# Sliding-window attention and a highway layer on one core: the order of issue changed at seven steps

## Chip, core and metric

The kernel runs on one core of a Trainium2 chip. The metric is the device time of one execution in microseconds (us); a lower time is better. Engines are named as in the profile: PE (TensorE), DVE (VectorE), ACT (ScalarE), POOL (GpSimd) and SP (SyncE). POOL and SP also issue the DMAs.

## What is computed

Attention with a causal window of 128 positions and an ALiBi bias, for 8 batches, 8 heads, 576 positions and 64 dimensions, then a highway layer on the 4608 x 512 result. Inputs and output are float32.

```python
scores = scale * np.matmul(q, k.transpose(0, 1, 3, 2))
mask = (rel >= 0) & (rel < window)                 # rel = query - key position, window = 128
scores = np.where(mask, scores + bias[None], -1e9) # bias = -slope(head) * |rel|
attn = exp(scores - max) / sum
x = attn @ v                                       # heads side by side: 4608 x 512
H = np.maximum(x @ w_h, 0.0)
T = 1.0 / (1.0 + np.exp(-(x @ w_t + b_t)))
out = T * H + (1.0 - T) * x
```

## The kernel before

**Attention** is done in 32 units (batch b, s, g): s picks heads 0 to 3 or 4 to 7, g the first or second half of the query tiles. A unit is six steps, each with a letter that the order string uses:

- `T` (line 184, DVE): transposes of q and of k, from the loaded buffer `ld` into `tr`. T (b, s, 0) is q, T (b, s, 1) is k, for both halves g.
- `s` (line 227, PE): scores into four PSUM banks. Always banks 0 to 3, so a unit's scores wait for the exponential of the unit before.
- `e` (line 244, ACT): exponential, PSUM to `p` in bf16.
- `m` (line 249, DVE): the mask product, `p` times exp(bias) with zeros outside the window. For three units the bias is added by PE instead (line 209).
- `p` (lines 260 to 281, PE): PV, the product with V and a column of ones, into two halves of a PSUM bank pair named in the string (4 or 6).
- `n` (lines 294 and 295, DVE): the normalisation, reciprocal and product, PSUM to `x`. It frees the banks that the PV step filled.

**The highway layer** is done in 36 blocks (b, i) of 128 rows; i is 0 to 3, and 4 in odd batches, for the first 64 rows of two batches. Its steps:

- `x` (321, PE) four transposes of `x` into PSUM, `c` (326, ACT) their copy to `xt`, `h` (331, PE) the product with w_h.
- `u` (DVE): relu and the subtraction of x, `uu` = max(h, 0) - x, from PSUM (347, "relu-sub" below). For 14 blocks ACT does the relu first (`r`, 338) and DVE subtracts in SBUF (344). It frees the bank of h.
- `z` (355, 357, PE) the product with w_t and the bias; for 12 blocks ACT puts the bias in PSUM (`w`, 368) and PE adds to it (`y`, 372).
- `a` (377, ACT) tanh; then 0.5 + 0.5 tanh, on ACT (`t`, 381) or for 11 blocks on DVE (`k`, 385, the "half-gate").
- `g` (390, DVE): the gate product, `uu` times the gate.
- `o` (394, POOL): the sum with x into `ot`; for two blocks on DVE (`q`, 399). `d` (406, 410, SP) stores it.

**Loads** (`L`, lines 130, 136, 140, 144) are all issued by POOL and turn float32 into bf16. A load ("t", b, s, w) brings q (w = 0) or k (w = 1) of four heads into one of 20 `ld` buffers. A load ("v", b, 2, tile) brings 128 key positions of V of batches b and b + 1, all heads, into `va`. PV of half g = 0 reads V tiles 0 to 2, that of g = 1 tiles 1 to 4. POOL does its sums and its load issues in one order.

**What sets the order.** A string written out by hand, `ORDER`, gives every step of the program. The loop below takes one letter at a time, hands it the next unit, block or load of that letter's own list, and issues its instructions. Each engine runs its share strictly in that order, and waits only for its data and buffers. `LOADS` is the order of the loads among themselves. Moving a letter in the string moves the step on its engine and nothing else.

```python
    do = dict(M=..., L=load, T=tr, S=setup, s=scores, e=soft, m=mask, p=pv, n=norm, x=x_tr, c=x_copy,
              h=mm_h, u=relu_sub, z=mm_z, a=tanh, t=to_gate, k=to_gate_v, r=relu, g=gate, o=add_x, d=store,
              w=bias, b=bias_rows, f=bias_copy, y=mm_y, q=add_x_v)
...
        for step in steps:
            what = by[step][at[step]]
            what = what if isinstance(what, tuple) else (what,)
            at[step] += 1
            if step in "spxhzwb":
                bank = int(next(steps))
                what += (bank,)
            do[step](*what)
```

Of the kernel before, what the change touches and what calls it, by code (L numbers as in the profile page):

```python
# [14 lines left out]
RELU_ACT = (0, 3, 5, 8, 9, 11, 12, 13, 17, 19, 20, 21, 26, 28)  # L15
GATE_DVE = (6, 7, 9, 15, 19, 23, 25, 26, 29, 32, 34)

LOADS = (0, 1, 3, 4, 6, 5, 2, 12, 11, 9, 13, 17, 10, 16, 8, 18, 7, 14, 15, 21, 19, 20, 22, 27, 26, 23, 25, 24, 30, 29, 31, 32, 33, 28, 34, 37, 39, 35, 40, 43, 44, 45, 46, 38, 36, 47, 48, 42, 41, 52, 56, 57, 50, 53, 58, 59, 51, 49, 55, 54)

BIAS_ACT = (8, 9, 14, 17, 20, 24, 30, 31, 32, 33, 34, 35)  # L20
ADD_DVE = (33, 35)
# [4 lines left out]
ORDER = (  # L26
    "SLLSMSLLLTLLTLs0LTLeLLTLMSms0Lp4LeLTLmLs0LTp6enLs0nLmx4Lex5Tp6cmcs0Lnz4b5eLTp6mas0tfnz4e"
    "Lh5mx6rh7cux5az6ucgtTp4oap6nLds0nLh4Th5eLx6x7uLLrs0Tcz4eumh5cmx6as0cuz7egTp4oh6anLtds0Lm"
    "rp4tLuez6ngz7gaotx6p4aLmdcs0x7eh6nToTp4Ltds0cLnmh7euz4kw6gux5aos0Tch7eLdTp4Lynrs0akmp4w7"
    "eyugnh6oaTx4rs0Ldtgcgp6gmx4Lz5cnex4LLLoLTp6cds0unz4eoLTp6ads0anoh5tTeh4dmz6rux7ah4kmcx5t"  # L30
    "p6ucgs0rnox5ez4TLdh6gLcmax7s0roTz5cw4Lgp6deuTyLts0naLaLgz4ueLTop6Tas0otdh5enh4dgux6oth7u"
    "cgx4w5dh6mctoyurTx4ap6dcms0z4euknh5agp6TtLos0th4neduz6rmLLx7ap4mcs0np6egx4kh5nocs0ruLdx4"
    "gw5p6LmcyenuLh4Tox6az7rmtLdp4ags0cgz7otneTz6odTx4aLds0cx5mah4w7uh6cgkeuyoup4gtds0maz6eon"
# [6 lines left out]
def lists():  # L40
# [7 lines left out]
    for b in range(NB):  # L48
# [5 lines left out]
        else:  # L54
            loads += ts[:2] + vs[:3] + ts[2:] + vs[3:]
    by = dict(L=[loads[i] for i in LOADS], T=trs, S=list(range(4)), M=list(range(NS)))
    by.update(b=[()], f=[()])
# [398 lines left out]
```

## Time and profile before

| | us |
|---|---|
| median of 3 runs | 149.89 (149.45 to 150.98) |
| the profiled execution, its own time | 149.37 |
| its span, first to last instruction | 147.5 |
| PE busy | 129.5 (88%) |
| DVE busy | 132.1 (90%) |
| ACT busy | 119.3 (81%) |
| POOL busy | 88.6 (60%) |

The granted TensorE clock was 1.00 throughout. A row of a time line gives start, length, engine, line, operation, tiles, shape and count, and in brackets how long the engine stood idle before it and what ended that. One instruction's record begins some 0.08 to 0.1 us before the end of the one ahead of it, so lengths of neighbours overlap. A row of the waits gives who waited for whom, the total in us, how many times, and the longest. A row of the DMA view gives the transfer, the queue that issued it, how many, the size, and the median time from issue to landing. The loads' queue is served in order: each load lands after the one issued before it.

### The profile page before, as it was taken

Reading aid. Unit: us, or ns where it says so; the run is one execution under the profiler, and the core shown is the slowest. Engines: PE = TensorE matmul, PEld = TensorE weight load, DVE = VectorE, ACT = ScalarE, POOL = GpSimd, SP = SyncE. Lnnn points to the kernel's source line nnn. Section 1 sums busy time; section 2 is a strip of 40 time slices with the busy share of each in tenths; the row PEclk is TensorE's granted clock in tenths of the full one; section 3 lists DMA queues with packets and bytes.
Section 4 is the critical chain, followed back from the end, with each engine's and each line's share of the span. In section 5 each row is a group of like instructions: output and inputs, shape, how many; then the busy total and the mean of one; then the engine's idle time right before and its main releaser. Section 6 shows DMA issues by size and latency. Waiting matters only on the chain.

```text
span 147.5 us, 5788 instructions
## 1 busy us (share of the span) xinstructions
PE 129.5 (88%) x2525; PEld 79.9 (54%) x2525; DVE 132.1 (90%) x226; ACT 119.3 (81%) x167; POOL 88.6 (60%) x102
## 2 busy tenths in 40 slices
PE   0475689999999989979998999999999999999960
PEld 0134565575656555655745556675657666555520
DVE  4965998699999999999999999999999999967881
ACT  5298466959999689659998999979998898899850
POOL 6968762169168561996199773459854115585640
PEclk9999999999999999999999999999999999999999
DMA  2999999999999999799999999989999021153544
GB/s 29 194 158 188 187 205 194 182 205 185 164 174 197 207 201 196 157 168 206 249 193 194 148 233 287 123 179 156 167 243 194 12 76 71 42 178 142 211 134 154
DMA packets 48233, 25.01 MB, mean 170 GB/s; under 512 B 38480, under 2 KB 39504, under 8 KB 48208
## 3 DMA queue, kind: packets, MB, share of 16 engines
q0 software_dynamic: 42960, 15.21, 98.2%
q1 hardware_dynamic: 5248, 9.44, 18.8%
q8 instruction: 19, 0.31, 0.9%
q14 instruction: 6, 0.05, 0.1%
HBM read 30.41 MB, written 9.44 MB: 270 GB/s over the span
## 4 chain that ended last, share of the span: by engine, by line
PE 44%; DMA 27%; DVE 19%; POOL 5%; issue 3%; POOLq 0%; DVEq 0%
DMA va<-in_v_dram 13%; PE ps L331 13%; DMA wH<-in_moe_w_h_dram 7%; PE ps L355 7%; PE ps L372 6%; DMA ld<-in_q_dram 6%; DVE tr L184 5%; DVE p L249 4%; PE ps L227 4%; PE ps L281 4%; PE ps L321 3%; DVE x L295 3%; PE ps L260 3%; DVE uu L390 2%; POOL ld L130 2%
## 5 line engine op out<-in xcount | busy, mean ns | idle before, releaser
L394 POOL TENSOR_TENSOR ot<-uu,x 128x512 f32<-128x512 bf16 x34 | 43.5, 1285 | 45.5 <-DVE uu L390 25.6
L244 ACT ACTIVATE p<-ps 128x1792 bf16<-128x1792 f32 (+1 forms) x32 | 50.0, 1562 | 11.3 <-PE ps L227 11.0
L184 DVE STREAM_TRANSPOSE tr<-ld 128x576 uint32<-128x576 uint32 x32 | 39.3, 1248 | 4.0 <-DMA ld<-in_q_dram 3.2
L331 PE MATMUL ps<-wH,xt 128*128 128x512 bf16 x144 | 35.9, 379 | 0.6 <-DVE uu L347 0.6
L249 DVE TENSOR_TENSOR p<-p,mt 128x1792 bf16<-128x1792 bf16 (+1 forms) x29 | 31.3, 1086 | 1.2 <-ACT p L244 1.2
L136 POOL DMA_DIRECT2D va<-in_v_dram x25 | 25.3, 1016 | 1.3 <-DMA va<-in_v_dram 1.3
L355 PE MATMUL ps<-wT,xt 128*128 128x512 bf16 x96 | 25.6, 390 | 0.0
L295 DVE TENSOR_TENSOR x<-ps,rd 128x512 bf16<-128x512 f32 (+1 forms) x32 | 24.3, 758 | 1.3
L377 ACT ACTIVATE tt<-ps 128x512 f16<-128x512 f32 x36 | 21.5, 603 | 2.7 <-PE ps L372 1.9
L326 ACT COPY xt<-ps 128x512 bf16<-128x512 bf16 x36 | 21.0, 587 | 2.7 <-PE ps L321 2.6
L227 PE MATMUL ps<-tr,tr 32*64 32x192 bf16 (+2 forms) x1280 | 20.0, 246 | 2.1 <-DVE tr L184 2.1
L331 PEld LDWEIGHTS <-xt 128*128 128x128 bf16 x144 | 13.1, 98 | 13.7 <-issue 0.6
L227 PEld LDWEIGHTS <-tr 32*64 32x64 bf16 x1280 | 16.4, 111 | 7.3 <-DVE tr L184 3.7
L347 DVE SCALAR_TENSOR_TENSOR uu<-ps,x 128x512 bf16<-128x512 f32 x22 | 15.0, 685 | 2.4 <-PE ps L331 2.3
L260 PE MATMUL ps<-va,p 128*128 128x65 bf16 x256 | 13.7, 198 | 3.7 <-DVE p L249 1.3
L260 PEld LDWEIGHTS <-p 128*128 128x128 bf16 x256 | 11.6, 100 | 8.7 <-DVE p L249 2.4
L381 ACT ACTIVATE tt<-tt 128x512 f16<-128x512 f16 x25 | 15.8, 635 | 0.1
L390 DVE TENSOR_TENSOR uu<-uu,tt 128x512 bf16<-128x512 bf16 x36 | 14.9, 427 | 0.2
L281 PE MATMUL ps<-va,p 64*64 64x65 bf16 x448 | 14.6, 200 | 0.0
L321 PE MATMUL ps<-ident,x 128*128 128x128 bf16 x144 | 13.9, 224 | 0.5 <-DVE x L295 0.4
L321 PEld LDWEIGHTS <-x 128*128 128x128 bf16 x144 | 10.2, 100 | 6.7 <-DVE x L295 0.7
L355 PEld LDWEIGHTS <-xt 128*128 128x128 bf16 x96 | 8.3, 99 | 8.2 <-issue 0.9
(46 smaller groups left out, 116.0 us busy)
## 6 DMA issues: line engine op xcount, KB each, us to landing
out_dram<-ot SPq DMA_DIRECT2D x32, 256.0 KB, 4.1
ld<-in_q_dram POOLq DMA_DIRECT2D x16, 288.0 KB, 7.6
ld<-in_k_dram POOLq DMA_DIRECT2D x16, 288.0 KB, 7.0
va<-in_v_dram POOLq DMA_DIRECT2D x12, 256.0 KB, 8.3
va<-in_v_dram POOLq DMA_DIRECT2D x11, 128.0 KB, 7.8
out_dram<-ot SPq DMA_DIRECT2D x8, 128.0 KB, 4.1
wT<-in_moe_w_t_dram POOLq DMA_DIRECT2D x1, 512.0 KB, 8.7
wH<-in_moe_w_h_dram POOLq DMA_DIRECT2D x1, 512.0 KB, 10.8
```

What stands on the lines that cost most here:

```text
L136: nc.gpsimd.dma_start(out=VA[b // 2][0:rows, h : h + n * H, m, 0:D], in_=v[b : b + n, :, m * P : m * P + rows].rearrange("b h p d -> p (b ...
L184: nc.vector.transpose(out=TR[i % NTR][:].rearrange("p s e -> p (s e)").bitcast(U32).rearrange("p (s t) -> p t s", t=NT), in_=LD[i % NLD][: ...
L227: nc.tensor.matmul(out=PS[r * D : r * D + D, bank + a, c0:c1], lhsT=KT[row : row + 32, k0 : k0 + D, e], rhs=QT[row : row + 32, q0 : q0 + c ...
L244: nc.scalar.activation(out=PB[i][:, :, 0:w], in_=PS[:, bank : bank + 4, 0:w], func=ACTF.Exp, scale=scale)
L249: nc.vector.tensor_tensor(out=p[:, :, 0:w], in0=p[:, :, 0:w], in1=MT[s][:, :, 448 - w : 448] if g else MT[s][:], op=ALU.mult)
L260: nc.tensor.matmul(out=PS[:, bank + o, a * E : a * E + E], lhsT=p[:, a, col : col + P], rhs=VA[b // 2][:, b % 2 * H + 4 * s + a, i, :], st ...
L295: nc.vector.tensor_tensor(out=X[b, g][:, s, :, 0:n, :], in0=av[:, :, 0:n, 0:D], in1=rd[:, :, 0:n, :].to_broadcast([P, 2, n, D]), op=ALU.mult)
L321: nc.tensor.transpose(out=XP[b, i][:, c * P : (c + 1) * P], in_=xchunk(b, i, c), identity=ident[:])
L331: nc.tensor.matmul(out=pa, lhsT=XT[b, i][:, c, :], rhs=wH[:, c, :], start=c == 0, stop=c == NC - 1)
L355: nc.tensor.matmul(out=pz, lhsT=xt[:, c, :], rhs=wT[:, c, :], start=c == 0, stop=False)
L377: nc.scalar.activation(out=tt[:], in_=PZ.pop((b, i)), func=ACTF.Tanh, scale=0.5)
L394: nc.gpsimd.tensor_tensor(out=like(ot[:], i), in0=like(UU.pop((b, i))[:], i), in1=xview(b, i), op=ALU.add)
```

## The change

Only the two constants change. The instructions, their number and their sizes stay as they are; PE, ACT and SP keep their order.

```diff
-LOADS = (..., 40, 43, 44, 45, 46, 38, 36, 47, 48, ...)
+LOADS = (..., 40, 43, 44, 38, 36, 45, 46, 47, 48, ...)
...
-    "rp4tLuez6ngz7gaotx6p4aLmdcs0x7eh6nToTp4Ltds0cLnmh7euz4kw6gux5aos0Tch7eLdTp4Lynrs0akmp4w7"
-    "eyugnh6oaTx4rs0Ldtgcgp6gmx4Lz5cnex4LLLoLTp6cds0unz4eoLTp6ads0anoh5tTeh4dmz6rux7ah4kmcx5t"
+    "rp4tLuez6ngmz7aotx6p4aLdcs0x7eh6ngToTp4Ltds0cLnmh7euz4ukw6gx5aos0Tch7eLdTp4Lynrs0akmp4w7"
+    "eyugnh6oaTx4rs0Ldtgcgp6mx4Lz5cnggex4LoLTp6cds0unz4eoLLLTp6ads0anoh5tTeh4dmz6rux7ah4kmcx5t"
```

Read out, this is on DVE, in three places:

| before | after |
|---|---|
| g (0,2), g (0,3), m (2,1,0), n (2,0,0), T (3,0,0) | g (0,2), m (2,1,0), n (2,0,0), g (0,3), T (3,0,0) |
| u (1,4), k (1,4), g (1,0), u (1,2), T (3,1,0) | u (1,4), u (1,2), k (1,4), g (1,0), T (3,1,0) |
| g (1,4), g (1,2), g (1,3), m (3,1,0), n (3,0,0), T (4,0,1) | g (1,4), m (3,1,0), n (3,0,0), g (1,2), g (1,3), T (4,0,1) |

and on POOL, in one:

| before | after |
|---|---|
| L t (5,0,0), L t (5,0,1), L t (5,1,0), L t (5,1,1), o (1,4), L v (4, tile 2), o (1,2), L v (4, tile 0), o (1,3) | L t (5,0,0), L t (5,0,1), o (1,4), L v (4, tile 2), o (1,2), L v (4, tile 0), L t (5,1,0), L t (5,1,1), o (1,3) |

## The prediction

> **What bounds the kernel now.** I read the page's busy shares, then the busy times by stretch, the waits of PE, the chain that ended last, and the time lines of DVE and POOL around each moved step, matching rows to steps by their order on each engine. Units are (batch, s, g), blocks (batch, i).
>
> ```profile
> PE 129.5 (88%) x2525; PEld 79.9 (54%) x2525; DVE 132.1 (90%) x226; ACT 119.3 (81%) x167; POOL 88.6 (60%) x102
> ...
> 36.00:54.00 18.00, 17.15 (x353) 10.36 (x352) 17.83 (x28) 15.85 (x22) 9.95 (x12) 1.00 1.65 187
> 54.00:66.00 12.00, 10.91 (x261) 7.16 (x260) 11.85 (x21) 9.17 (x13) 8.73 (x11) 1.00 1.13 176
> 66.00:78.00 12.00, 11.62 (x220) 6.81 (x217) 11.85 (x19) 11.76 (x18) 7.63 (x8) 1.00 1.45 215
> 78.00:87.00 9.00, 8.86 (x157) 5.31 (x158) 8.45 (x15) 8.48 (x12) 7.00 (x9) 1.00 2.10 177
> 87.00:142.00 55.00, 55.00 (x1012) 33.68 (x1010) 51.63 (x96) 49.23 (x74) 30.62 (x27) 1.00 0.80 151
> ```
>
> The columns are stretch, length, then PE, PEld, DVE, ACT, POOL. From 87 to 142 us PE never rests, so whatever PE gains before 87 moves the end one for one, and nothing more can be gained after it. From 36 to 78 it is DVE that hardly rests (17.83+11.85+11.85 = 41.53 of 42 us), and PE idles 2.32 us (0.85+1.09+0.38). All the edits lie there. PE's waits:
>
> ```profile
> PE ps L260 <- DVE x L295: 1.1, 1, 1.1
> PE ps L331 <- DVE uu L347: 0.6, 1, 0.6
> PE ps L260 <- DMA va<-in_v_dram: 0.5, 1, 0.5
> ```
>
> In time: 0.61 at 53.32, where the W_h product of block (1,3) needs the bank that relu-sub (1,2) frees; 1.07 at 64.21, where PV (3,1,0) needs the bank that the normalisation of (3,0,0) frees; 0.52 at 78.14, where PV (4,0,0) waits for V. The chain shows the last:
>
> ```profile
> 66.53 11.56 DMA va<-in_v_dram
> 78.09 0.05 issue
> 78.14 0.42 PE ps L260 x8
> ```
>
> The DVE and POOL time lines show something else, the length of two mask products:
>
> ```profile
> 44.11 0.75 DVE L390 TENSOR_TENSOR uu<-uu,tt 128x512 bf16<-128x512 bf16 x2
> 44.78 2.04 DVE L249 TENSOR_TENSOR p<-p,mt 128x1792 bf16<-128x1792 bf16 x1
> ...
> 59.99 1.06 DVE L390 TENSOR_TENSOR uu<-uu,tt 128x512 bf16<-128x512 bf16 x3
> 60.98 2.04 DVE L249 TENSOR_TENSOR p<-p,mt 128x1792 bf16<-128x1792 bf16 x1
> ...
> 75.28 1.06 DVE L249 TENSOR_TENSOR p<-p,mt 128x1792 bf16<-128x1792 bf16 x1
> ...
> 44.61 1.26 POOL L394 TENSOR_TENSOR ot<-uu,x 128x512 f32<-128x512 bf16 x1 [1.64 <-DVE uu L390]
> ...
> 75.50 1.88 POOL L394 TENSOR_TENSOR ot<-uu,x 128x512 f32<-128x512 bf16 x1
> ```
>
> The mask products at 44.78 and 60.98 take 2.04, that at 75.28 takes 1.06. At 44 the first gate product starts POOL's sum, the second holds it off until 44.86, the sum runs to 45.87 and the mask product ends 0.95 later. At 75 the mask product follows its gate product at once, is not delayed, and the POOL sum takes 1.88 instead: it ends 1.03 after the mask product. So whichever comes first makes the other wait, about 1.0 us.
>
> **The change part by part.** Times are those of the profiled execution (149.37 us, span 147.5, 1.87 around it), which is 0.52 below the median of 149.89.
>
> Mask (2,1,0) ahead of gate (0,3). It follows gate (0,2) at 44.45, 0.16 ahead of the POOL sum, as at 75, so 1.08 instead of 2.04. Its exponential ended at 44.15. DVE then stands until PV (2,0,0) ends on PE at 45.94: the normalisation (2,0,0) ends at 46.92, not 47.67. Gate (0,3) comes behind it; DVE leads by 0.41. POOL's sum (0,2) pays: done at 46.50, not 45.87, and the load of V (2,tile 3) queued behind it is issued 0.64 late.
>
> Normalisation (2,0,0) ahead of gate (0,3): PV (2,1,0), at 47.72 right after x ended at 47.67, starts 0.15 earlier.
>
> Relu-sub (1,2) ahead of half-gate (1,4) and gate (1,0): 0.20+0.33 earlier, plus the lead of 0.41, so its bank is free at 52.3 instead of 53.27. The 0.61 wait goes and PE stands about 0.9 ahead. What is late next: PV (2,0,1), at 54.18, needs V (2,tile 3):
>
> ```profile
> va<-in_v_dram POOLq DMA_DIRECT2D x1, 256.0 KB, 8.3
> ```
>
> Issued at 45.82, it lands at 54.1, 0.1 before its use. PE gets 0.08 of the 0.9, and the issue is 0.64 later now. The load before it lands at 51.3 (42.42+8.9), 2.8 earlier, against some 1.9 to 2.4 from landing to landing for V of batch 4 in a full queue, so 54.1 may hold; bounds 54.1 and 54.75. I take 54.1. PE: -0.08. Gate (1,0) ends 0.2 later, which only its sum on POOL sees, idle 2.92 before it.
>
> Mask (3,1,0) and normalisation (3,0,0) ahead of gates (1,2), (1,3). The mask product starts at 59.9 (60.33 less the lead). At 1.08 it ends at 61.0. The normalisation then waits for PV (3,0,0) on PE (ends 61.42) and ends at 62.66 instead of 64.15; here the lead from 44 us is spent. PV (3,1,0) starts when PE is ready, 62.97: -1.24. The two gates follow, to 63.3; transpose (4,0,1) starts at 63.22 (was 64.07), so DVE is 0.85 ahead. Next late: PV (3,0,1), which needs normalisation (3,1,0), 65.85 instead of 66.70. PE falls back to -0.85, and both engines keep that to 77.
>
> Two loads of batch 5 behind V of batch 4. POOL: two issues of 0.55 leave the place ahead of sum (1,4), V (4,tile 2), sum (1,2) and V (4,tile 0). Sum (1,4), ready at 59.97, runs 60.92 to 61.95; V follows at 61.9 (was 63.98), the other V, behind sum (1,2), at 64.2 (was 66.53), the loads at 65.4 and 65.9. Their buffers were last read before 11 us, so nothing else stands in the way. Landings now: 69.7 (60.46+9.2), 71.7, 73.8 for the two moved loads, 76.2 and 78.1 for V. With the same spacing and the queue 0.43 early (its first load follows sum (1,1)): V at 71.6 and 73.5, the loads at 75.5 and 77.6. Their transposes were at 78.01 and 80.58, now due 0.85 earlier, 77.16 and 79.73: covered by 1.7 and 2.1. PV (4,0,0) no longer waits: PE is through with its last product at 76.7. PE: -0.85-0.52, and 0.07 of overlap at the seam, -1.44. Without the load move V would still be at some 77.7, and most of this gone: the loads carry about 1.0 of the sum.
>
> From 78 on PE is 1.44 ahead and DVE 0.85. DVE stood 0.29 and 0.17 for PE at 84.43 and 85.29, so it catches up; no bank that it frees (80.00 for 82.04, 83.80 for 85.02, each less 0.85) comes late. From 86 us everything is moved alike. V (4,tile 3) lands at 86.6 (78.17+8.4), due at 86.84. Sum: 149.89-1.44 = 148.45; with ends: V (2,tile 3) late by 0.64, a gain of 0.7; all three waits gone after 54, 1.75 with the seams.
>
> A rule from the Trainium skill bears on the second mask product. That row is odd: no POOL sum runs until 62.05, only two load issues (60.98 to 62.07), yet it ends 0.95 after them. SBUF — State Buffer, "SBUF: two separate sides", says that VectorE and GpSimd share a port pair as an exclusive lock, held for the whole instruction, and that GpSimd writes the descriptors of its own DMAs through it. By that the mask product in its new place would wait for the issues at 59.5 to 60.6, end at 61.55, and the sum would be 148.6; the rows bear it out once, and the gate products at 60.33 and 60.65, 0.41 each under such issues, speak against it. It is the mild form of rival 2.
>
> **The rivals.**
> 1. V (2,tile 3) follows its issue and lands at 54.75. PE is 0.6 late at PV (2,0,1); the 1.07 at 64 absorbs it; PV (3,0,1) is 0.2 early and with 0.52 the end 0.72: 149.2. For it: the 2.8 above. Against: the V issued at 99.33 took 6.7.
> 2. Load issues hold up the mask product whatever its place, by the full 1.0: it ends at 62.0, the normalisation at 63.2, DVE is only 0.3 ahead: 149.1. For: the second 2.04. Against: the product at 41.93 ran 1.08 under two issues.
> 3. The gain is given back at 110. V (6,tile 0), issued at 100.49, lands at 110.1, and PV (6,0,0) begins at 110.12:
>
> ```profile
> va<-in_v_dram POOLq DMA_DIRECT2D x1, 256.0 KB, 9.6
> ```
>
> If it doesn't move, PE stops there and nothing is left: 149.9. For: the 9.6. Against: the load before the batch-6 V took 5.2 from its issue, so the queue was nearly empty and follows POOL, whose issues follow DVE's gates, which follow PE.
> 4. The other side, slower: V (2,tile 3), late from its issue, takes as long as that 9.6. It lands at 56.1, PE is 1.9 late, 64 and 78 give back 1.4: 150.4. It decides from a landing at about 55.5. At 10.6 it is over 1%.
>
> **How the numbers follow.** Forecast 0.50; rival 1 0.12, rival 2 0.10, rival 3 0.13, rival 4 or a loss like it 0.15. The time is the forecast's, 148.45, given as 148.5, its own range 148.0 to 149.0. The range 147.9 to 150.2 reaches over rivals 1 to 3 and a part of 4. A measurement of this kernel tells about 1% (1.5 us) from no change; 148.39 is that bound, so half of the forecast is faster: 0.25. Slower by over 1%: most of rival 4, 0.13. Within 1%: 0.62.
>
> **What would show it.** Mask products near 44.5 and 60 at 1.08, and POOL's sum at 44.6 near 1.9. No PE wait on x near 63 nor on V near 77; a new one on V near 54. Normalisation (3,0,0) at 61.5 behind an idle DVE. PE without gaps from 87 to its end near 140.9; a wait on V near 109 is rival 3. A wait of a transpose near 77 would mean that the moved loads came too late, which I costed at nothing.

## The result, and the profile after

The changed kernel takes 148.62 us (median of 22 runs, 147.73 to 153.3), the kernel before 149.79 beside it (22 runs, 148.57 to 151.44): ratio 0.9931, 95% interval [0.991, 0.9952]. The ratio is taken over the executions of each kernel that lie within 1.5% of its fastest, so it is not exactly the ratio of the two medians. By the ratio the change gains 1.0 us, by the medians 1.2 us. That is within the 1% (1.5 us) that the prediction named as the least that can be told from no change, but the interval lies clear of 1: the changed kernel is faster, by less than 1%.

The profiled execution took 149.08 us (span 147.3). Its waits of PE between 36 and 147 us (who waited for whom, total, times, longest):

```profile
PE ps L260 <- DVE x L295: 0.6, 1, 0.6
PE ps L260 <- DMA va<-in_v_dram: 0.4, 1, 0.4
PE ps L355 <- issue: 0.3, 2, 0.2
PE ps L281 <- issue: 0.2, 1, 0.2
PE ps L331 <- issue: 0.2, 1, 0.2
```

The three waits of before are gone. The first row is new, at 66.84 (normalisation (3,1,0)), the second too, at 54.96 (V (2, tile 3)). The rows of L355 and L331 are no stops: 31 of 2525 products have no record in this trace, and each such gap is one product of 0.16 long. The row of L281 is a real stop, at 78.46; the last section takes it up.

Time lines of DVE, then of POOL, around the first and the third place:

```profile
45.14 0.41 DVE L390 TENSOR_TENSOR uu<-uu,tt 128x512 bf16<-128x512 bf16 x1
45.47 1.08 DVE L249 TENSOR_TENSOR p<-p,mt 128x1792 bf16<-128x1792 bf16 x1
47.01 0.21 DVE L294 RECIPROCAL rd<-ps 128x8 f32<-128x8 f32 x1 [0.46 <-PE ps L281]
...
60.59 0.41 DVE L390 TENSOR_TENSOR uu<-uu,tt 128x512 bf16<-128x512 bf16 x1
60.93 1.06 DVE L249 TENSOR_TENSOR p<-p,mt 128x1792 bf16<-128x1792 bf16 x1
62.23 0.23 DVE L294 RECIPROCAL rd<-ps 128x12 f32<-128x12 f32 x1 [0.24 <-PE ps L281]
...
45.64 1.93 POOL L394 TENSOR_TENSOR ot<-uu,x 128x512 f32<-128x512 bf16 x1 [1.64 <-DVE uu L390]
47.52 1.20 POOL L136 DMA_DIRECT2D va<-in_v_dram  x1
...
60.55 0.54 POOL L130 DMA_DIRECT2D ld<-in_q_dram  x1
61.06 0.55 POOL L130 DMA_DIRECT2D ld<-in_k_dram  x1
61.61 1.40 POOL L394 TENSOR_TENSOR ot<-uu,x 128x512 f32<-128x512 bf16 x1
```

Both mask products take 1.08 and 1.06 where they took 2.04, and behind each DVE stands for PE. POOL's sum at 45.64 pays (1.93 for 1.26), so the issue of V (2, tile 3) comes at 47.52, and the chain that ended last runs through just that:

```profile
45.64 1.88 POOL ot L394
47.52 7.40 DMA va<-in_v_dram
55.63 0.97 PE ps L372 x4
```

Busy time by stretch (length, PE, PEld, DVE, ACT, POOL):

```profile
36.00:54.00 18.00, 17.56 (x394) 11.14 (x398) 17.24 (x30) 16.32 (x23) 10.37 (x12) 1.00 1.63 179
54.00:66.00 12.00, 11.42 (x261) 7.46 (x263) 11.61 (x21) 10.28 (x14) 9.32 (x11) 1.00 1.23 181
66.00:78.00 12.00, 11.16 (x228) 7.01 (x229) 11.84 (x19) 11.39 (x18) 7.38 (x9) 1.00 1.46 219
```

DVE has slack of 0.76 in the first stretch and 0.39 in the second, where it had 0.17 and 0.15; in the third it is still the full engine.

To compare two traces step by step, one has to start where the change starts: the last untouched step, PV (1,1,1) at 43 us, begins 1.02 later in this execution than in that of before, in code that is the same (over all traces of this study that offset runs from -0.32 to +1.20). From there on, this is the gain of PE, cumulated, in us:

| start of | predicted | measured |
|---|---|---|
| PV (2,1,0) | 0.15 | 0.27 |
| h (1,3) | 0.9 | 0.95 |
| the step behind PV (2,0,1) | 0.08 | 0.35 |
| PV (3,1,0) | 1.24 | 1.65 |
| PV (3,0,1) | 0.85 | 0.93 |
| PV (4,0,0) | 1.44 | 1.62 |
| the step behind it | 1.44 | 1.24 |
| PE's end | 1.44 | 1.26 |

A second profiled execution of the changed kernel gives the same at PV (3,1,0), PV (3,0,1) and PV (4,0,0), to 0.01. Behind them PE stops for longer than in the first, and 0.70 is left at its end. So the steps repeat from one execution to the next; the gain left at the end does not.

### The profile page after: what moved, and what is told of

Read it like the earlier page. It is cut to its first block, busy times and chain, and to the rows that moved or that the text cites. A ratio compares the mean times of both kernels' runs of the same rounds, so it can differ in the third digit from the quotient of the medians.

```text
span 147.3 us, 5759 instructions
## 1 busy us (share of the span) xinstructions
PE 127.8 (87%) x2494; PEld 80.5 (55%) x2525; DVE 130.5 (89%) x226; ACT 119.6 (81%) x167; POOL 88.5 (60%) x102
## 4 chain that ended last, share of the span: by engine, by line
PE 67%; DVE 11%; DMA 11%; POOL 5%; issue 3%; POOLq 0%; DVEq 0%
PE ps L331 19%; PE ps L355 11%; PE ps L227 8%; PE ps L372 7%; PE ps L281 7%; DMA ld<-in_q_dram 5%; PE ps L321 5%; PE ps L260 5%; DMA va<-in_v_dram 5%; DVE x L295 3%; PE ps L357 3%; DVE tr L184 3%; POOL va L136 2%; POOL ld L130 2%; DVE p L249 1%
## 5 line engine op out<-in xcount | busy, mean ns | idle before, releaser
L331 PE MATMUL ps<-wH,xt 128*128 128x512 bf16 x132 | 34.9, 379 | 0.8 <-issue 0.2
L249 DVE TENSOR_TENSOR p<-p,mt 128x1792 bf16<-128x1792 bf16 (+1 forms) x29 | 29.4, 1020 | 1.4 <-ACT p L244 1.4
L355 PE MATMUL ps<-wT,xt 128*128 128x512 bf16 x80 | 23.9, 389 | 1.2 <-issue 0.5
L331 PEld LDWEIGHTS <-xt 128*128 128x128 bf16 x144 | 13.1, 98 | 13.1
L281 PE MATMUL ps<-va,p 64*64 64x65 bf16 x448 | 14.9, 200 | 0.2 <-issue 0.2
L355 PEld LDWEIGHTS <-xt 128*128 128x128 bf16 x96 | 8.3, 98 | 8.1 <-issue 0.7
## 6 DMA issues: line engine op xcount, KB each, us to landing
wH<-in_moe_w_h_dram POOLq DMA_DIRECT2D x1, 512.0 KB, 10.7
```

Of the source, the lines that this page charges most:

```text
L249: nc.vector.tensor_tensor(out=p[:, :, 0:w], in0=p[:, :, 0:w], in1=MT[s][:, :, 448 - w : 448] if g else MT[s][:], op=ALU.mult)
L281: nc.tensor.matmul(out=PS[orow : orow + D, bank + o, a * E : a * E + E], lhsT=p[row : row + D, a, col : col + D], rhs=VA[b // 2][row : row ...
L331: nc.tensor.matmul(out=pa, lhsT=XT[b, i][:, c, :], rhs=wH[:, c, :], start=c == 0, stop=c == NC - 1)
L355: nc.tensor.matmul(out=pz, lhsT=xt[:, c, :], rhs=wT[:, c, :], start=c == 0, stop=False)
```

## The experiments

The question is which part carries the 1.0 us, and whether by the steps named. Call the first two places of DVE's order P, the third Q, the load move L. Four runs do them singly or two at a time; two more complete the table. Each result is the ratio to the kernel before, with its 95% interval. The theory was the prediction's chain: Q frees 1.2 us, without L the late V of batch 4 takes nearly all of it back, P gives little. The rival was that the parts add up.

**P alone**, against the kernel before:

```diff
-    "rp4tLuez6ngz7gaotx6p4aLmdcs0x7eh6nToTp4Ltds0cLnmh7euz4kw6gux5aos0Tch7eLdTp4Lynrs0akmp4w7"
+    "rp4tLuez6ngmz7aotx6p4aLdcs0x7eh6ngToTp4Ltds0cLnmh7euz4ukw6gx5aos0Tch7eLdTp4Lynrs0akmp4w7"
```

> Only the two DVE places at 44 and 52 us (mask (2,1,0), normalisation (2,0,0), relu-sub (1,2)); nothing at 60, loads as before. Theory (each step passes its lead on only as far as the next thing that is late): mask (2,1,0) 1.08 us instead of 2.04, DVE 0.4 ahead at 48, PE 0.9 ahead at 53 and back to 0.1 at PV (2,0,1), which stands for V tile 3 in its middle; mask (3,1,0) still 2.04; the lead of 0.4 runs through to 78 because the loads of batch 4 are issued 0.4 earlier: 0.4 us faster, ratio 0.997. Rival (every PE wait that goes is worth its length): 0.6 to 0.75 us faster, ratio 0.995.

Measured 0.9992 [0.9956, 1.0029]. In the trace the mask product takes 1.09, PE gains 0.94 up to h (1,3) and keeps 0.38 at the end: about DVE's own lead, 0.41, survives. The times don't show it: the interval holds no change as well as the theory's 0.997, and just leaves out the rival's 0.995.

**Q alone**:

```diff
-g (1,4), g (1,2), g (1,3), m (3,1,0), n (3,0,0), T (4,0,1)
+g (1,4), m (3,1,0), n (3,0,0), g (1,2), g (1,3), T (4,0,1)
```

> Only the DVE place at 60 us (mask (3,1,0), normalisation (3,0,0) ahead of two gates), loads as before. Theory: mask 1.08 instead of 2.04, normalisation waits for PE, PV (3,1,0) 1.2 us earlier, 0.8 of it left at PV (3,0,1); then PV (4,0,0) waits 1.3 us for V, which lands at 78.1 as before, and nearly all is gone: 0 to 0.1 us faster, ratio 1.000. Rival (every PE wait that goes is worth its length): 1.07 us faster, ratio 0.993.

Measured 1.0089 [1.0047, 1.013]: slower, which neither expected. Time lines of DVE and POOL:

```profile
65.18 1.48 DVE L344 TENSOR_TENSOR uu<-rr,x 128x512 bf16<-128x512 bf16 x1
66.58 0.22 DVE L294 RECIPROCAL rd<-ps 128x12 f32<-128x12 f32 x1
...
64.64 1.19 POOL L394 TENSOR_TENSOR ot<-uu,x 128x512 f32<-128x512 bf16 x1
65.74 1.20 POOL L136 DMA_DIRECT2D va<-in_v_dram  x1
```

The mask product takes 1.07 and PV (3,1,0) starts 1.23 earlier, as expected. But relu-sub (2,0) takes 1.48, not 0.41: it is held up by the sum and, beyond the sum's end at 65.83, for some 0.4 by the load issue behind it (it ends at 66.66, and takes 0.41 itself). Normalisation (3,1,0) follows late and PE waits 1.91 for it. In the trace PE's loss is then absorbed in the wait for V (net 0.0); the seven timings say +1.3 us, so this one execution does not show the whole loss. The granted clock of each execution shows where more of it comes from: four of the seven have a mean of 0.979 to 0.984 and took 151.27 to 151.63, the other three, the profiled one among them, 0.991 to 1.000 and 149.94 to 150.44. No execution of the kernel before, beside them, is under 0.989. So in most executions the clock also fell; the trace of the next run shows such a fall at a stop of PE.

**L alone**:

```diff
-L t (5,0,1), L t (5,1,0), L t (5,1,1), o (1,4), L v (4, tile 2), o (1,2), L v (4, tile 0), o (1,3)
+L t (5,0,1), o (1,4), L v (4, tile 2), o (1,2), L v (4, tile 0), L t (5,1,0), L t (5,1,1), o (1,3)
```

> Only the two loads of batch 5 behind V of batch 4. Theory: V lands near 74, PV (4,0,0) doesn't wait, 0.5 us faster, ratio 0.997; mask (3,1,0): if load issues hold it up, it is now behind one issue only (till 61.0) but meets the sum of block (1,4), so still about 2.0. Rival (the loads are worth what they carry in the whole change, about 1.0): ratio 0.993.

Measured 1.0124 [1.0079, 1.017]: slower too. DVE and POOL:

```profile
59.59 3.35 DVE L390 TENSOR_TENSOR uu<-uu,tt 128x512 bf16<-128x512 bf16 x3
62.85 1.08 DVE L249 TENSOR_TENSOR p<-p,mt 128x1792 bf16<-128x1792 bf16 x1
...
60.06 0.55 POOL L130 DMA_DIRECT2D ld<-in_k_dram  x1
60.60 1.18 POOL L394 TENSOR_TENSOR ot<-uu,x 128x512 f32<-128x512 bf16 x1
61.70 1.20 POOL L136 DMA_DIRECT2D va<-in_v_dram  x1
62.92 2.02 POOL L394 TENSOR_TENSOR ot<-uu,x 128x512 f32<-128x512 bf16 x1
```

The three gate products at 60 take 3.35, not 1.06 as before: the third, gate (1,3), lasts from 60.24 to 62.93. Nothing on DVE moved; POOL's sum (1,4) did, from 62.05 to 60.60, onto the gates. The mask product behind is then quick (1.08), but comes late, and PE waits 2.39 for normalisation (3,0,0). Next the granted clock falls (stretch, length, PE, PEld, DVE, ACT, POOL, then the clock):

```profile
63.00:65.00 2.00, 0.00 (x0) 0.10 (x1) 1.97 (x4) 0.89 (x2) 2.00 (x2) 0.95 0.92 141
65.00:66.00 1.00, 0.88 (x16) 0.73 (x15) 1.00 (x2) 0.00 (x0) 1.00 (x1) 0.50 1.01 152
66.00:68.00 2.00, 1.98 (x57) 1.51 (x55) 1.75 (x5) 0.51 (x1) 2.00 (x4) 0.50 1.35 220
68.00:70.00 2.00, 1.80 (x11) 0.94 (x10) 1.09 (x1) 1.71 (x3) 0.36 (x1) 0.50 1.82 247
```

From 65 to past 71 us PE runs at 0.50. Against the kernel before, PE is 1.20 late at PV (3,1,0), 3.01 at PV (3,0,1) and 3.15 at its end: the stop costs 1.2, the slow clock most of the rest.

**Q and L without P** (the changed kernel with P undone):

```diff
-    "rp4tLuez6ngmz7aotx6p4aLdcs0x7eh6ngToTp4Ltds0cLnmh7euz4ukw6gx5aos0Tch7eLdTp4Lynrs0akmp4w7"
+    "rp4tLuez6ngz7gaotx6p4aLmdcs0x7eh6nToTp4Ltds0cLnmh7euz4kw6gux5aos0Tch7eLdTp4Lynrs0akmp4w7"
```

> The DVE place at 60 us and the loads, without the places at 44 and 52. Theory: 0.8 kept at PV (3,0,1) and 0.5 at PV (4,0,0): 1.25 us faster, ratio 0.992, so nearly the whole change; more than its two parts alone (0 to 0.1 and 0.5). Rival (parts add up): the sum of the two runs beside it.

Measured 0.9958 [0.9927, 0.9989]: a gain, from two parts that each lose alone, though less than the 0.992 expected. The mask product takes 1.06, relu-sub (2,0) 0.53, and PV (4,0,0) does not wait for V.

**P and Q without L**, against the changed kernel:

```diff
-L t (5,0,1), o (1,4), L v (4, tile 2), o (1,2), L v (4, tile 0), L t (5,1,0), L t (5,1,1), o (1,3)
+L t (5,0,1), L t (5,1,0), L t (5,1,1), o (1,4), L v (4, tile 2), o (1,2), L v (4, tile 0), o (1,3)
```

> The changed kernel without the move of the two loads (the DVE moves alone, all three places). Theory (the mask product and normalisation free 1.2 at 64, but V of batch 4 then still lands near 77.5, so PV (4,0,0) waits about 1.2 for it and nearly all is given back): ratio to before 0.998 to 1.000. If relu-sub (2,0) is also held up by a sum and by the issue of V (4, tile 0) behind it, as in the run of the third place alone: 1.003 to 1.009. Rival (the parts add up): 0.997.

Measured 1.0019 [0.9986, 1.0052]. Relu-sub (2,0) takes 1.49 under the same sum and issue as with Q alone, PE waits 1.92 at PV (3,0,1), and V, landing at 77.61, is then not waited for. For that case 1.003 to 1.009 was expected; the interval reaches into it, the middle lies below. In three of the 12 executions the mean clock is 0.981 or 0.982, in the others 0.990 or more, so part of the distance to Q alone can be how often the clock fell.

**P and L without Q**:

```diff
-g (1,4), m (3,1,0), n (3,0,0), g (1,2), g (1,3), T (4,0,1)
+g (1,4), g (1,2), g (1,3), m (3,1,0), n (3,0,0), T (4,0,1)
```

> The changed kernel without the moves of the third place: mask product (3,1,0) stays behind gates (1,2) and (1,3), the loads and the first two places are moved. Theory (POOL's sum (1,4) and the issue of V (4, tile 2) now fall on the gates and hold gate (1,3) up, as in the run of the loads alone): gate (1,3) takes 2 to 2.7 instead of 0.41, PE waits over 1.5 for x near 64, ratio to before 1.003 to 1.012. Rival (the loss of the loads alone came from the granted clock that fell there, and from DVE being late; with the 0.4 lead of the first places it does not come): 0.994 to 0.998.

Measured 1.0117 [1.0082, 1.0153]. Gate (1,3) takes 2.69 again, PE waits 2.39, and the clock falls to 0.50 again. The lead of P does not help. The table (ratio to before):

| | without P | with P |
|---|---|---|
| neither Q nor L | 1 | 0.9992 |
| Q | 1.0089 | 1.0019 |
| L | 1.0124 | 1.0117 |
| Q and L | 0.9958 | 0.9931 |

The parts do not add up: Q and L undo each other's damage. L takes two issues of 0.55 out of the way, so that POOL's sum (1,4) and the issue of V come earlier. With Q the sum then falls on the end of the mask product and on normalisation (3,0,0), which reads PSUM and is held up in no trace here; without Q it falls on gate (1,3), which is. Without L the sum (1,2) and the issue behind it come later (64.84 with P and Q, 64.18 in the changed kernel), fully onto relu-sub (2,0). Two runs test these two explanations.

**L and P, the issue of V ahead of the sum.** Is it the sum or the load issue that holds gate (1,3)? Against the run before:

```diff
-L t (5,0,1), o (1,4), L v (4, tile 2), o (1,2)
+L t (5,0,1), L v (4, tile 2), o (1,4), o (1,2)
```

> The run without the third place, with the issue of V (4, tile 2) ahead of sum (1,4) on POOL instead of behind it, so that no sum stands between the issues at 60 and at 61. Theory (load issues hold up DVE's products like sums do): gate (1,3) is still held up, from 60.9 into the issue of V that begins near 61.1, so it takes over 1 us. Rival (only a sum can hold it up): gate (1,3) takes 0.41, and only the mask product behind it can still be late. The ratio to before is below the 1.0117 of that run by either, since the mask product comes 0.6 to 1.6 earlier: 0.995 to 1.005.

```profile
60.05 2.03 DVE L390 TENSOR_TENSOR uu<-uu,tt 128x512 bf16<-128x512 bf16 x3
62.01 2.36 DVE L249 TENSOR_TENSOR p<-p,mt 128x1792 bf16<-128x1792 bf16 x1
...
60.53 0.55 POOL L130 DMA_DIRECT2D ld<-in_k_dram  x1
61.05 1.19 POOL L136 DMA_DIRECT2D va<-in_v_dram  x1
62.22 3.15 POOL L394 TENSOR_TENSOR ot<-uu,x 128x512 f32<-128x512 bf16 x2
```

Gate (1,3) takes 1.38, from 60.71 to 62.09, and only load issues run on POOL beside it; the first sum starts at 62.22. So an issue alone can hold up a product. (The mask product then meets the sums and takes 2.36.) The Trainium skill, SBUF — State Buffer, "SBUF: two separate sides", says that whoever starts first on the port pair which the two engines share keeps it for the whole instruction, and that GpSimd needs the pair to write its descriptors; but against a VectorE instruction with two SBUF inputs it gives this lock only to a GpSimd instruction that reads SBUF. If an issue only writes, gate (1,3), a product of two SBUF inputs, would by that not have waited; this run does not agree, with 1.38 for 0.41. Whether an issue also reads SBUF, no run here shows. Nor does every issue hold a product: the mask product at 60.93 in the changed kernel takes 1.06, though two issues of q and k run from 60.55 to 61.61. The time, 1.0058 [1.0014, 1.0102], is just above the range expected for it.

**P and Q without L, relu-sub (2,0) behind the normalisation**, against the run of P and Q:

```diff
-u (2,0), n (3,1,0), T (4,1,0)
+n (3,1,0), u (2,0), T (4,1,0)
```

> The changed kernel without the move of the two loads, as in the run before last of that kind, and relu-sub (2,0) behind normalisation (3,1,0). Theory (what the DVE moves alone lose at 66 comes from relu-sub (2,0), held up for 1.1 by a sum and a load's issue while the normalisation stands behind it): the normalisation ends near 65.9 instead of 68.0, PE's wait at 66 to 68 falls from 1.9 to under 0.3, and PV (4,0,0) then waits 0.5 to 1.2 for V of batch 4, which still lands near 77.6; ratio to before 0.993 to 0.997, against 1.0019. Rival (the normalisation or the transpose behind it is held up instead): 0.999 to 1.003.

```profile
65.40 0.41 PE L260 MATMUL ps<-va,p 128*128 128x65 bf16 x8 [0.46 <-DVE x L295]
...
77.54 0.42 PE L260 MATMUL ps<-va,p 128*128 128x65 bf16 x8 [1.28 <-DMA va<-in_v_dram]
```

PE's wait at PV (3,0,1) falls from 1.92 to 0.46 (under 0.3 was expected): relu-sub (2,0) was the cause of that wait. And the V of batch 4, landing at 77.49, now stops PE for 1.28. The gain left in the trace is 0.30, the ratio 0.9982 [0.9943, 1.0021], its middle just outside the 0.993 to 0.997 expected. So what the prediction said of L, that without it V takes most of the gain back, is shown here, on an arrangement where nothing else takes it first. The edit itself is not shown to save time: the intervals of the two runs overlap, and PE's gain at its end is 0.29 without the edit and 0.30 with it, since without it the wait for V absorbs the loss.

**Two repairs.** The traces point to two leftovers in the changed kernel: the stop at 54.96 for V (2, tile 3), and the wait of 0.6 at 66.84. First, on POOL, against the changed kernel:

```diff
-o (0,2), L v (2, tile 3)
+L v (2, tile 3), o (0,2)
```

> The changed kernel with one POOL step moved: the load of V (2, tile 3) is issued ahead of sum (0,2) instead of behind it. Theory (the 0.9 that PE gains by the earlier relu-sub (1,2) is lost because this load is issued late): it is issued near 46.4 instead of 47.5 and lands near 53.8, PV (2,0,1) does not stop in its middle (0.42 in the changed kernel), PE keeps its lead there; DVE, which leads by 0.4 only, is late next at normalisation (3,1,0), so 0.0 to 0.3 us faster than the changed kernel, ratio to before 0.991 to 0.993. Rival (the queue, not the issue, sets the landing): V lands at 54.9 all the same, no change, 0.993.

Measured 0.995 [0.9921, 0.9978]; the middle is above the 0.991 to 0.993 expected. V is issued at 43.28, not near 46.4, since POOL stands idle there, and lands at 53.54. Counted from PV (1,1,1), the issue comes 3.67 earlier than in the changed kernel and the landing 0.81, so the rival is right in part: the queue sets most of the landing. PV (2,0,1) does not stop; but PE's gain, 0.65 at h (1,3), is 0.41 at 59 us all the same, as in the run of P alone. That stop cost next to nothing in the end: DVE, not V, sets PE's place there.

Second, on DVE, against the changed kernel:

```diff
-u (2,0), n (3,1,0), T (4,1,0)
+n (3,1,0), u (2,0), T (4,1,0)
```

> The changed kernel with relu-sub (2,0) behind normalisation (3,1,0) on DVE instead of ahead of it. Theory (after the edits DVE, not PE, is late at PV (3,0,1), which waits 0.58 for that normalisation): the normalisation ends 0.4 to 0.5 earlier, the wait falls to about 0.15, PE is 0.35 to 0.4 ahead from 67 on, ratio to before 0.990 to 0.991. Rival (the lead is lost again in the stall of PE near 78, or at a later wait for DVE): under 0.1 us, 0.993.

Measured 0.9914 [0.988, 0.9948]. The wait at 66 is gone, PE's list of waits has one row left, and PE gains 1.67 from 43 us to its end, where the changed kernel gains 1.26 in one trace and 0.70 in the other:

```profile
PE ps L260 <- DMA va<-in_v_dram: 0.3, 1, 0.3
```

The changed kernel once more, without an edit:

> The changed kernel itself once more, beside the next one on the same chip, so that the two can be set against each other. Ratio to before 0.993 by its earlier runs (0.991 to 0.9952); the theory of PE's stops at fixed places in its instruction stream expects that its stop inside PV (4,0,0) or at x (3,3) comes and goes from run to run, since it was there in three kernels' traces and missing in two others.

Beside it both repairs, against the changed kernel:

```diff
-o (0,2), L v (2, tile 3)
+L v (2, tile 3), o (0,2)
...
-u (2,0), n (3,1,0), T (4,1,0)
+n (3,1,0), u (2,0), T (4,1,0)
```

> Both repairs: load of V (2, tile 3) ahead of sum (0,2), and relu-sub (2,0) behind normalisation (3,1,0). Theory (the first repair takes PE's stop at 54 away, but DVE, which leads by 0.4 only, then holds PE at 57 to 59, so nothing of it is left; the second is worth the 0.4 to 0.6 of PE's wait at 66): ratio to before 0.989 to 0.992, about 0.4 us below the changed kernel. Rival (the stop at 54 costs its 0.4 to the end): 0.986 to 0.988, about 0.8 us below the changed kernel.

The changed kernel measured 0.9928 [0.989, 0.9965] (median 148.61), both repairs 0.9942 [0.9897, 0.9987] (149.01). In the trace of both repairs PE has no wait for data left after 36 us and gains 1.65. The theory's 0.4 does not show in the time: 12 executions each, spread over 2 to 4 us, can't tell apart the medians 148.61 of the changed kernel, 148.63 of the second repair and 149.01 of both. No version measured here is shown to beat the changed kernel.

## Why the prediction was right, point by point

The time, 148.5 forecast and 148.62 measured, came by the steps named, with the differences below. That it is so close is in part luck: the kernel before measured 149.79 this time, 0.10 under the value that the sum starts from, and the gain was forecast at 1.44 and came to 1.0 by the ratio, 1.2 by the medians, and 1.26 and 0.70 in the two traces.

**First two places.** The mask product (1.08 forecast and measured), POOL's sum (about 1.9, measured 1.93), DVE's lead (0.41; 0.42) and the 0.9 of PE at h (1,3) (0.95) are as forecast. The term at PV (2,0,1) was mis-sized: 0.08 kept by the prediction, 0.35 measured. The prediction kept the landing of V where it was, though its issue was to come 0.64 later. Counted from PV (1,1,1), the issue came 0.68 later and the landing 0.20 earlier (7.4 from issue to landing, not 8.3). The repair run shows that this term does not count: without the stop, the gain falls to DVE's 0.3 to 0.4 all the same. The prediction made V the limit there; it was DVE.

**Third place.** Mask product 1.06 (1.08), normalisation (3,0,0) behind an idle DVE, as forecast; the step frees 1.23 at PV (3,1,0) (1.16). The fall back to DVE's lead at PV (3,0,1), 0.85 forecast, came to 0.93, and the wait of 0.58 there is the one the prediction named as next.

**Loads.** V of batch 4 was forecast at 71.6 and 73.5 and landed at 73.63 and 76.05, in an execution that began 1.0 late. The issues came when the forecast has them, counted from PV (1,1,1) (61.94 and 64.27 against 61.9 and 64.2), but the loads took 10.7 and 10.8, not 9.7 and 9.3. The load ahead of them did not land the 0.43 earlier that the prediction took for the whole queue, and from landing to landing it was 2.7 and 2.4, not 2.4 and 1.9. The cover shrank from 3.2 to 1.5 us (76.05 against 77.54) and that of the two moved loads from 1.7 and 2.1 to 0.8 and 1.8; none was used up. PV (4,0,0) started 1.62 ahead without a wait (1.44). That the loads carry about 1.0 came true in size: PE's end gains 1.26 with them and 0.29 without. The way there was partly another, as in that run relu-sub (2,0) takes the gain before V can.

**What it did not have.** Of the 1.62, the first trace loses 0.38 by a stop inside PV (4,0,0), the second 0.17 there and 0.75 further on, for which the profile names no wait for data; in the first the rest stays to the end, as forecast. And the prediction did not see how narrowly the parts fit. It priced the load move as a gain on top of the DVE moves and named no case in which a sum or an issue that comes at a new time falls on a gate product or on relu-sub (2,0). The runs with L or Q alone lose 1.2% and 0.9% by just that, and by the fall of the clock that comes with it. The forecast held because both are in the change, not because each step is a gain.

**The rivals.** V (2, tile 3) late (1): no, it landed 0.20 earlier, counted as above; the stop of 0.42 is the one that the forecast itself has, and the repair run shows that it cost next to nothing. Load issues holding the mask product (2): not at this mask product, 1.06 under two issues; but gate (1,3), one product earlier in the old order, was held by issues alone in the run made for it. The milder form, 148.6, was worked out by the Trainium skill's lock without its condition, that against such a product it stands only for an instruction that reads SBUF (above); so it does not follow from there. V (6, tile 0) giving all back (3): it landed at 108.06, 2.0 earlier than before (3.0 counted from PV (1,1,1)). A very late V (4): no.

## What to carry to other kernels

An operation that is off the path still has neighbours on the other engine: before moving work on POOL, list what DVE will be running at the new time, and put there what reads PSUM or transposes rather than SBUF-to-SBUF products. Test a reorder of two engines as a whole and in its parts; here two losing halves make the gain. And compare traces from the point where the change begins, since the untouched start differed by up to 1.5 us between executions.

## What the runs showed of the hardware

**Load issues hold up DVE.** A gate product of 0.41 took 1.38 beside issues alone and 2.69 beside issue, sum and issue (in both traces with L and without Q), and relu-sub (2,0) 1.48 and 1.49 beside sum and issue. In these five cases the product ended 0.91 to 1.23 after the start of an issue of V that took 1.19 to 1.20; less its own 0.41, it was let go some 0.5 to 0.8 into that issue (an estimate). Transposes, normalisations and relu-sub from PSUM were not held up in any of the 14 traces (transposes 1.22 to 1.26, normalising products of 512 columns 0.69, relu-sub from PSUM 0.67 to 0.69). What decides who goes first is open: of the products at 60 us the first two went through in every trace, under the same issues, and at most a later one was held; and the two gates at 63.37 in the changed kernel took 0.75 together while the issue of V ran from 62.96 to 64.16.

**The clock fell around a stop of 2.39 us.** PE stood 2.39 in both runs with L and without Q, and the granted clock went to 0.50, for 6.8 and 3.4 us; in the profiled execution of the run with the issue ahead of the sum it stood 2.36 and the clock stayed at 1.00. It fell at 64.80, 2.07 into the stop, in one trace, and at 66.88, 1.22 after the stop had ended, in the other. In all 14 traces the clock's changes lie a whole number of steps of 3.41 us apart (1, 2, 12, 23, 35 or 36 of them). Laid on that grid, one step holds 2.07 and 2.19 of the two stops that brought a fall, but only 1.23 of the 2.36, and 1.60 and 1.39 of the 1.91 and 1.92 in the runs with Q and without L. That fits a clock that is decided once a step by how long PE stood in it, somewhere between 1.60 and 2.07, and it would explain why the same kernel meets the fall in some executions and not in others: in the run with the issue ahead of the sum, nine of the 12 have a mean clock of 0.987 or less, three of 0.992 to 0.995. No run moved the stop on the grid, so it is argued, not shown. The Trainium skill, TensorE: Matmul & The Clock Gate, "Part 1: The HAM clock gate (the "warmup" mystery)", gives an idle window of about 3.4 us ahead of the lower state; here less was enough, 2.07.

**PE stops at fixed places.** Stops that the profile calls "issue" fell inside a group of equal products, in some executions and not in others. PE rows of the changed kernel:

```profile
77.88 0.37 PE L281 MATMUL ps<-va,p 64*64 64x65 bf16 x8
78.46 0.25 PE L281 MATMUL ps<-va,p 64*64 64x65 bf16 x4 [0.21 <-issue]
```

of its second profiled run:

```profile
84.10 0.33 PE L321 MATMUL ps<-ident,x 128*128 128x128 bf16 x3
85.06 0.22 PE L321 MATMUL ps<-ident,x 128*128 128x128 bf16 x1 [0.62 <-issue]
```

of the run with both repairs:

```profile
52.26 0.53 PE L227 MATMUL ps<-tr,tr 32*64 32x192 bf16 x25
53.05 0.34 PE L227 MATMUL ps<-tr,tr 32*64 32x192 bf16 x15 [0.27 <-issue]
```

and of that with the issue ahead of the sum:

```profile
73.80 0.28 PE L281 MATMUL ps<-va,p 64*64 64x65 bf16 x6
74.49 0.34 PE L281 MATMUL ps<-va,p 64*64 64x65 bf16 x10 [0.40 <-issue]
```

Counted in PE's order of products these are numbers 1374, 1502, 862 and 1246 (the first by its step, as records are missing ahead of it), all a multiple of 128 apart, and each stop begins 1.0 to 1.2 us after the end of a packet of the queue that the profile page lists as

```profile
q8 instruction: 19, 0.31, 0.9%
```

which is 16 KB a packet, one for about every 130 products. Two more traces stop at numbers 862 and 1502 (first repair) and 1502 (Q and L without P), 1.0 to 1.6 us after such a packet. That fits a wait for PE's own instructions, of 0.2 to 0.6 us a time. No run here changed that queue or the length of the stream, so it is argued, not shown. Whatever their cause, such stops are one reason why gains of 0.4 us in a trace need not be seen again in the times.
